# Building the key and query stacks of an attention kernel through DRAM: six stores and eight loads a unit in place of 24 pieces

## The chip, the cores and the metric

The kernel runs on one core of one Trainium2 chip. The metric is the device time of one execution in microseconds (us), the median of several runs. The profile is one execution taken by the hardware profiler; its span runs from the first instruction to the last. The engines are named as in the profile: PE (matrix multiplication; PEld its weight loads), DVE (vector), ACT (scalar functions), POOL (GpSimd) and SP, which here only issues DMA transfers. "SPq" is SP's queue of such issues.

## The reference, cut to what matters

One block of a transformer on x of 2048 tokens by 1024 columns. The part that matters is the first half, causal attention in four segments of 512 tokens, with a running memory from segment to segment, 32 heads of 32 columns:

```
q, k, v = LN(x) @ wq, LN(x) @ wk, LN(x) @ wv        # then cut into 32 heads, 4 segments of L = 512
for s in range(4):
    logits = einsum("bhqd,bhkd->bhqk", q[s], k[s]) * scale + causal mask
    a_dot  = softmax(logits) @ v[s]
    a_mem  = (phi(q[s]) @ M) / (phi(q[s]) @ z)
    o[s]   = g * a_mem + (1 - g) * a_dot
    M, z   = M + phi(k[s]).T @ v[s],  z + sum(phi(k[s]))
h  = x + concat(o) @ wo
h2 = h + gelu(LN(LN(h)) @ w1 + b1) @ w2 + b2
```

Everything is float32.

## The kernel before, in words

Matrix products are made with operands that are split into a high and a low part (names ending in h and l; the low part is the value less the high part), so that a product is three matmuls: high by high, low by high, high by low (`mm3`, lines 114 to 117).

The attention is done in two halves of two segments each. In a half the loop of lines 648 to 664 runs over 8 groups of 4 heads and, in each, over the two segments: 16 units a half, 32 in all. A unit is one call of `dense` (line 402): the projections of keys, queries and values for one group of heads and one segment, each 8 steps of three matmuls of 512 columns (lines 115 to 117). The tiles have the 128 columns of the group, 32 for each head, as partitions, and the 512 tokens as columns. While a unit's projections run, the four heads of the unit before are worked off: `interleave` (line 661) takes one step of `heads` after each step of `dense`. The steps of one head are written out in `PLAN` (line 31): `q` is the product of queries and keys (`qk`, line 533), `n` the normalisation of the softmax on POOL, `t` the transposes, `a` the product with the values, `s` and `o` subtractions and sums. The first step of a head's slot is a `q`, so the first `q` of a unit's heads follows the first step of the next unit's key projection.

The product of queries and keys is one matmul over 96 partitions: for head j a tile `ks` of 96 rows holds the head's 32 rows of kh, of kl and of kh again, and a tile `qs` holds qh, qh and ql, so that the sum over 96 rows is kh qh + kl qh + kh ql (line 541). These are the stacks. `stack` (line 372) makes the four tiles of a unit, called for the keys at the first step of the query projection (line 420) and for the queries at the first step of the value projection (line 435). kh and qh come from ACT (lines 413 and 427), kl and ql from DVE (lines 414 and 428). The tiles `ks` and `qs` have five buffers each: of the four tiles of a unit the first takes a free one, and each of the others waits until the product of queries and keys of one head of the unit before has read its buffer.

In the kernel before, each 32 rows of a stack tile are a DMA of its own from SBUF to SBUF (line 377): 4 tiles of 3 pieces for the keys, and the same for the queries, 24 pieces of 64 KB in a unit.

All DMAs around the change are issued on SP, whose queue runs in order: the pieces; the weights of the next groups (`load_block`, line 326, 512 KB each, two buffers; a buffer comes free when POOL or DVE has made the low part of the weights before it); the finished output rows of a group (line 609, `o_dram`, 256 KB each, from a tile of 128 by 512); at the end of a half those rows read back (line 683, `orr`), weights of the output projection (line 700) and rows of x (line 696). An instruction waits on SP for what it depends on, and all behind it waits too.

The program is written in a tile framework. It finds the dependences between instructions, tiles in DRAM included, and at build time a planner fixes the order of each engine's instructions and of each queue: it walks through the program with costs of its own and takes the earliest written instruction whose inputs it expects to be there. Around the attention only the opening (line 286) has its order written out by hand; elsewhere an instruction or a transfer may stand ahead of one that was written earlier but that the planner expects to be held up.

Of the kernel before, what the change touches and what calls it, by code (L numbers as in the profile page):

```python
# [10 lines left out]
F32 = mybir.dt.float32  # L11
# [6 lines left out]
P = 128  # L18
# [21 lines left out]
def raw(ap):  # L40
    return ap.bitcast(F32)


def build(tc, x, wq, wk, wv, wo, beta, w1, b1, w2, b2, out):
    nc = tc.nc
    top = ExitStack()
    const = top.enter_context(tc.tile_pool(name="const", bufs=1))
    dram = top.enter_context(tc.tile_pool(name="dram", bufs=1, space=DRAM))
# [33 lines left out]
    p1_dram = [dram.tile([P, 512], F32, name=f"p1_dram{j}") for j in range(FB // 2)]  # L82
    h_dram = [[dram.tile([S // P, P, FB // 4, P], F32, name=f"h_dram{i}{s}") for s in range(2)] for i in range(2)]

    acts = {}

    def split(pool, w, hi, lo, hi_eng="vector", lo_eng="gpsimd"):
# [99 lines left out]
    def hooked(gen, fn, every, count):  # L187
        for n, _ in enumerate(gen):
            if n % every == every - 1 and n // every < count:
                fn(n // every)  # L190
            yield
# [152 lines left out]
    def attention(half, first):  # L344
# [26 lines left out]

        def stack(a, b, name, order):
            out = []
            for j in range(4):
                st = ab.tile([96, 512], F32R, tag=name, name=name, bufs=5)
                for blk, src in enumerate(order):
                    nc.sync.dma_start(raw(st[32 * blk:32 * blk + 32, :]), raw((a, b)[src][32 * j:32 * j + 32, :]))
                out.append(st)
            return out

# [21 lines left out]
        def dense(g, sl, ws, u):  # L402
# [15 lines left out]
            for c in project(ws["q"], sl, "qps", qps):  # L418
                if c == 0:
                    u["ks"] = stack(kh, kl, "ks", (0, 1, 0))  # L420
                if c == 2 and s < 3:
                    zc = ab.tile([P, 64], F32, name="zc", bufs=2)[:, 0:1]
                    pk = phi_sum(kparts, "pk", zc)
                next(behind, None)
                yield
# [7 lines left out]
            for c in project(ws["v"], sl, "vps", vps):  # L433
                if c == 0:
                    u["qs"] = stack(qh, ql, "qs", (0, 0, 1))
                if s > 0:
                    if c == 2:
                        pq = phi_sum(qparts, "pq")
                    if c == 4:
                        while small:  # L440
                            one_small()
                        pqh, pql = tmpr("pqh"), tmpr("pql")
                        mzh = ab.tile([P, 256], F32R, name="mzh", bufs=1)[:, 0:132]
                        mzl = ab.tile([P, 256], F32R, name="mzl", bufs=1)[:, 0:132]
                        nc.scalar.copy(pqh, pq)
                        nc.gpsimd.tensor_copy(mzh, MZ[:, g, :])
                        nc.gpsimd.tensor_tensor(mzl, MZ[:, g, :], raw(mzh), op=ALU.subtract)
                    if c == 5:
                        nc.gpsimd.tensor_tensor(pql, pq, raw(pqh), op=ALU.subtract)
                if c == 1 and s < 3:  # L450
                    pkn = ps_dense("pkn")
                    for i in range(4):
                        nc.tensor.transpose(pkn[:, i * P:(i + 1) * P], pk[:, i * P:(i + 1) * P], ident)
                    pkh, pkl = tmpr("pkh"), tmpr("pkl")
                    nc.scalar.copy(pkh, pkn)
                if c == 2 and s < 3:
                    nc.vector.tensor_tensor(pkl, pkn, raw(pkh), op=ALU.subtract)
                next(behind, None)
                yield
# [188 lines left out]
        for g in range(NG):  # L648
            for sl in range(2):
                u = {"g": g, "s": 2 * half + sl}  # L650
                d = dense(g, sl, ws, u)
# [6 lines left out]
                else:  # L658
                    if g == NG - 1 and sl == 1:
                        d = hooked(d, lambda k: load_o(half, 0, k, ab), 3, NG - 1)  # L660
# [19 lines left out]
    def load_o(half, sl, g, tp):  # L680
        oh, ol = o_tiles(half, sl)
        orr = tp.tile([P, 512], F32, tag="tmp", name="orr", bufs=5)
        nc.sync.dma_start(orr, o_dram[2 * half + sl][g])
        hi, lo = oh[:, g, :], ol[:, g, :]
        if sl == 0 and g % 2 == 0:
            nc.vector.tensor_copy(hi, orr)
        else:
            op = nc.scalar.copy(hi, orr)
            if sl == 1:
                tc.add_manual_dep(op.ins, acts["mm"].ins.name, NOSYNC, reason="program order")  # L690
        (nc.vector if g % 2 else nc.gpsimd).tensor_tensor(lo, orr, raw(hi), op=ALU.subtract)
# [613 lines left out]
    for half in range(2):  # L1305
# [53 lines left out]
        order = ExitStack()  # L1359
# [84 lines left out]
```

## Time and profile before

| what | value |
|---|---|
| runs | 2302.54, 2304.96, 2303.82 us; median 2303.82 us |
| span of the profiled execution | 2296.2 us; the median of the runs is 7.6 us above it |
| PE busy | 2270.4 us, 99% of the span |
| DVE, ACT, POOL busy | 67%, 53%, 48% |
| granted clock of PE | 1.000 |
| attention, half 0 | about 30 to 500 us, then its output projection |
| attention, half 1 | about 900 to 1375 us, then its output projection |
| transfers on SP's queue | 316.40 MB, 45.4% of the 16 DMA engines' time over the span |
| pieces of the stacks | 768, 64.0 KB each, median 2.0 us from issue to landing |

The profile gives no time for its own execution other than the span; what lies around it is taken from the median of the runs. A share of busy time is a mean over stages. The rows that name a line group all instructions of that line: how often, how long, and how long the engine idled ahead of them. The ends of matmuls are modelled, since matmuls are pipelined: their starts follow each other faster than their durations say.

### The profile page before, as it was taken

What the parts mean: (1) busy time and instruction counts of PE and PEld (TensorE: products, weight loads), DVE (VectorE), ACT (ScalarE), POOL (GpSimd) and SP (SyncE); (2) the same over time, 40 slices, a digit from 0 to 9 for tenths busy, and PEclk for the clock granted to TensorE, in tenths of its full rate; (3) what the DMA queues carried; (4) which work ended last, traced back from release to release, by engine and by line L of the source; (5) the groups of instructions that cost most, each with busy time, mean ns of one, the idle gap of its engine ahead of it and who ended that gap; (6) DMA issues with size and microseconds to landing.
All of it is one profiled execution on the core that took longest, in us unless ns stands there. A gap on an engine that the chain in (4) does not pass through costs nothing.

```text
span 2296.2 us, 35279 instructions
## 1 busy us (share of the span) xinstructions
PE 2270.4 (99%) x11769; PEld 1890.8 (82%) x11769; DVE 1540.3 (67%) x3173; ACT 1225.0 (53%) x2549; POOL 1092.4 (48%) x1134
## 2 busy tenths in 40 slices
PE   8999999999999999999999999999999999999999
PEld 6888888878888888888888887888888888888887
DVE  6777777776655565777777777565566766577563
ACT  6777777775453445777777776363344223322221
POOL 5545555555244442555555556253445554155430
PEclk9999999999999999999999999999999999999999
DMA  6333333345465654433333344466667976476762
GB/s 190 92 85 91 93 89 85 87 120 182 139 204 172 188 165 142 113 91 86 85 87 88 87 111 140 156 211 175 176 188 263 345 243 216 159 253 221 249 234 90
DMA packets 322719, 355.36 MB, mean 155 GB/s; under 512 B 26190, under 2 KB 218730, under 8 KB 322538
## 3 DMA queue, kind: packets, MB, share of 16 engines
q1 hardware_dynamic: 259370, 316.40, 45.4%
q10 hardware_dynamic: 63168, 36.71, 5.3%
q8 instruction: 93, 1.52, 0.3%
q14 instruction: 88, 0.72, 0.1%
HBM read 226.59 MB, written 76.09 MB: 132 GB/s over the span
## 4 chain that ended last, share of the span: by engine, by line
PE 91%; ACT 3%; POOL 2%; DVE 2%; issue 1%; DMA 1%; ACTq 0%; SPq 0%; POOLq 0%; DVEq 0%
PE po L1278 22%; PE bps L882 9%; PE cps L882 7%; PE dps L882 6%; PE po L593 6%; PE ppt L573 6%; PE pqk L541 3%; PE vps L116 2%; PE vps L115 2%; PE kps L115 2%; PE kps L116 2%; PE vps L117 2%; PE kps L117 2%; PE pwo L117 2%; PE pwo L116 2%; PE pwo L115 2%
## 5 line engine op out<-in xcount | busy, mean ns | idle before, releaser
L557 POOL TENSOR_SCALAR pr<-pr,nm,gate 128x128 f32<-128x128 f32 (+3 forms) x512 | 322.6, 639 | 345.9 <-DVE nm L554 260.0
L550 ACT ACTIVATE pr<-pr,mx 128x256 f32<-128x256 f32 (+3 forms) x512 | 287.6, 562 | 161.9 <-DVE mx L542 158.2
L580 DVE TENSOR_TENSOR ptl<-ppt,pth 128x512 fp32r<-128x512 f32 (+1 forms) x384 | 227.2, 599 | 86.2 <-ACT pth L575 82.0
L542 DVE CUSTOM_DVE_ANT_0 pr<-pqk,mask 128x256 f32<-128x256 f32 (+3 forms) x512 | 243.3, 484 | 46.5 <-PE pqk L541 43.7
L573 PE MATMUL ppt<-ident,pr 128*128 128x128 f32 x1280 | 223.6, 277 | 2.1 <-POOL pr L557 1.4
L575 ACT CAST pth<-ppt 128x512 fp32r<-128x512 f32 (+1 forms) x384 | 194.2, 517 | 39.0 <-PE ppt L573 33.1
L1288 DVE TENSOR_TENSOR c<-c,po 128x512 f32<-128x512 f32 x160 | 105.4, 683 | 143.1 <-PE po L1278 135.5
L573 PEld LDWEIGHTS ppt<-ident,pr 128*128 128x128 f32 x1280 | 164.6, 140 | 32.5 <-POOL pr L557 2.6
L541 PE MATMUL pqk<-ks,qs 96*128 96x256 f32 (+3 forms) x512 | 161.3, 315 | 0.0
L92 POOL TENSOR_TENSOR wl<-wr,wh 128x1024 fp32r<-128x1024 f32 x52 | 124.5, 2393 | 70.8 <-PE pqk L541 27.6
L593 PE MATMUL po<-pth,vs 128*64 128x512 f32 (+3 forms) x512 | 155.4, 326 | 0.3 <-ACT pth L575 0.2
L593 PE MATMUL po<-ptl,vs 128*64 128x512 f32 (+3 forms) x512 | 153.9, 310 | 1.3 <-DVE ptl L580 1.2
L1278 PE MATMUL po<-w2h,zh 128*128 128x512 f32 x378 | 121.1, 390 | 0.8 <-DVE zh L1218 0.4
L1135 POOL TENSOR_TENSOR w2r<-w2r 128x512 f32<-128x512 f32 x54 | 85.4, 1593 | 72.0 <-DVE c L1288 36.9
L541 PEld LDWEIGHTS pqk<-ks,qs 96*128 96x128 f32 x512 | 96.2, 188 | 21.5
L994 POOL TENSOR_TENSOR s<-r 128x512 f32<-128x512 f32 x28 | 43.6, 1559 | 143.4 <-DVE sa L1010 87.1
L882 PE MATMUL bps<-zh,sb 128*128 128x512 f32 x336 | 111.0, 391 | 0.0
L882 PE MATMUL bps<-zh,sa 128*128 128x512 f32 x336 | 110.8, 390 | 0.0
L115 PE MATMUL vps<-yh,wh 128*128 128x512 f32 x256 | 109.4, 427 | 0.9 <-DVE MZ L497 0.9
L115 PE MATMUL kps<-yh,wh 128*128 128x512 f32 (+1 forms) x264 | 110.1, 417 | 0.0
L115 PE MATMUL qps<-yh,wh 128*128 128x512 f32 x256 | 106.8, 417 | 0.0
L1278 PE MATMUL po<-w2h,hl 128*128 128x512 f32 x322 | 103.2, 390 | 0.5 <-POOL hl L1218 0.3
(241 smaller groups left out, 6657.1 us busy)
## 6 DMA issues: line engine op xcount, KB each, us to landing
hr<-h_dram SPq DMA_DIRECT2D x112, 448.0 KB, 5.4
w2r<-in_B_w SPq DMA_DIRECT2D x122, 256.0 KB, 4.4
r<-in_B_w SPq DMA_DIRECT2D x56, 512.0 KB, 4.5
h_dram<-ht ACTq DMA_DIRECT2D x84, 256.0 KB, 3.7
ks<-kh SPq DMA_DIRECT2D x256, 64.0 KB, 2.0
qs<-qh SPq DMA_DIRECT2D x256, 64.0 KB, 2.0
wr<-in_A_wo SPq DMA_DIRECT2D x32, 512.0 KB, 4.0
wx<-in_B_w SPq DMA_DIRECT2D x56, 256.0 KB, 3.5
```

The lines of the kernel that those rows point to most:

```text
L115: nc.tensor.matmul(ps, ah, bh, start=first, stop=False)
L116: nc.tensor.matmul(ps, ah, bl, start=False, stop=False)
L541: nc.tensor.matmul(pqk[:, :n], u["qs"][j][:, i * P:(i + 1) * P], u["ks"][j][:, 0:n], start=True, stop=True)
L542: nc.vector.tensor_tensor_reduce(out=st["pr"][:, offs[i]:offs[i] + n], in0=pqk[:, :n], in1=mask[:, 512 - n:512], op0=ALU.add, op1=ALU.min, ...
L550: nc.scalar.activation(pi, pi, AF.Exp, bias=mx[:, i:i + 1], scale=-1.0, accum_out=mx[:, 4 + i:5 + i])
L557: nc.gpsimd.tensor_scalar(pi, pi, nm[:, 4 + k:5 + k], gate[:, 1, 4 * g + j:4 * g + j + 1], op0=ALU.mult, op1=ALU.mult)
L573: nc.tensor.transpose(ppt[:, o:o + P], pr[:, offs[i] + jk * P:offs[i] + (jk + 1) * P], ident)
L575: acts["pth"] = n, nc.scalar.copy(pth[:, base:base + w], ppt[:, :w])
L580: nc.vector.tensor_tensor(o, x0, x1, op=ALU.subtract)
L593: nc.tensor.matmul(po[:, P * jk:], v, st[part][:, koff[jk]:koff[jk] + w], start=(jk, part) == (0, "pth"), stop=(jk, part) == (2, "ptl"))
L882: nc.tensor.matmul(ps, x_[:, c, :], y_[:, c, :], start=first and c == 0 and n == 0, stop=last and c == 3 and n == 2, skip_group_check=True)
L1278: nc.tensor.matmul(ps, x_[:, k], y_[k], start=opens and k == 0 and i == 0, stop=closes and k == self.KP - 1 and i == 2, skip_group_check=True)
```

## The change

Four tiles in DRAM are added, two for the key stacks and two for the query stacks, used in turn. Each holds 128 rows of 3 parts of 512 columns, laid by row, then part, then column. `stack` first stores the three parts of all four heads, each with one DMA of 128 rows of 2 KB (256 KB, rows 6 KB apart in DRAM). Then each tile of 96 rows is loaded with one DMA: 32 rows of 3 parts lie together in DRAM, so that it is one stretch of 192 KB. In the tile, row 3r + p now holds part p of row r, where it was row 32p + r; keys and queries are permuted alike. Each load depends on all three stores. The calls of `stack` stay where they are, and all 14 transfers are issued on SP.

```diff
+    s_dram = {n: [dram.tile([P, 3, 512], F32, name=f"{n}_dram{k}") for k in range(2)] for n in ("ks", "qs")}
     acts = {}
...
         def stack(a, b, name, order):
             out = []
+            n = acts[name] = acts.get(name, 0) + 1
+            d = s_dram[name][n % 2]
+            for blk, src in enumerate(order):
+                nc.sync.dma_start(d[:, blk], raw((a, b)[src]))
             for j in range(4):
                 st = ab.tile([96, 512], F32R, tag=name, name=name, bufs=5)
-                for blk, src in enumerate(order):
-                    nc.sync.dma_start(raw(st[32 * blk:32 * blk + 32, :]), raw((a, b)[src][32 * j:32 * j + 32, :]))
+                nc.sync.dma_start(raw(st), d[32 * j:32 * j + 32].rearrange("r b n -> (r b) n"))
                 out.append(st)
             return out
```

## The prediction

> **What bounds the kernel now.** I read the page first: the span, the busy shares, the chain of work that ended last, and the group of the matmuls that read the stacks.
>
> ```profile
> span 2296.2 us, 35279 instructions
> ...
> PE 91%; ACT 3%; POOL 2%; DVE 2%; issue 1%; DMA 1%; ACTq 0%; SPq 0%; POOLq 0%; DVEq 0%
> ...
> L541 PE MATMUL pqk<-ks,qs 96*128 96x256 f32 (+3 forms) x512 | 161.3, 315 | 0.0
> ```
>
> PE carries 91% of the chain, DMA 1%. The last figure of the third row is what matters here: the 512 matmuls that read the stacks left PE idle before them for 0.0 us in all. A stack never comes late today. Then the windows, cut by stage: two rows of start, attention of half 0 and its end, and the start, attention and end of half 1. The columns are the window, its length, the busy time of PE, of its weight loads, of DVE, ACT and POOL (instructions in brackets), the granted clock, the DMA engines' share and GB/s.
>
> ```profile
> 0.00:30.00 30.00, 20.36 (x119) 17.74 (x119) 21.53 (x45) 17.34 (x24) 18.00 (x37) 1.00 0.73 223
> 30.00:60.00 30.00, 29.55 (x169) 24.47 (x168) 20.94 (x55) 20.38 (x50) 14.95 (x22) 1.00 0.57 159
> 60.00:480.00 420.00, 419.07 (x2554) 354.66 (x2554) 312.65 (x925) 305.09 (x774) 214.92 (x302) 1.00 0.34 87
> 480.00:560.00 80.00, 76.01 (x418) 61.21 (x417) 58.76 (x142) 53.71 (x119) 48.17 (x54) 1.00 0.46 143
> 920.00:960.00 40.00, 39.08 (x239) 32.86 (x240) 29.20 (x88) 26.65 (x69) 24.61 (x32) 1.00 0.46 126
> 960.00:1320.00 360.00, 360.00 (x2202) 305.35 (x2201) 273.04 (x813) 266.12 (x673) 203.44 (x267) 1.00 0.34 87
> 1320.00:1420.00 100.00, 96.32 (x561) 78.86 (x560) 75.97 (x205) 74.11 (x175) 54.19 (x67) 1.00 0.38 111
> ```
>
> PE is busy 419.07 of 420 us and 360.00 of 360 us in the two stretches where nearly all stacks are made, at full granted clock. In the stages that hold stacks (30 to 560 and 920 to 1420) PE idles 0.45 + 0.93 + 3.99 + 0.92 + 0.00 + 3.68 = 10.0 us. That is all that any change of these copies could win while PE's work stays as it is. The 9.6 us idle of the first 30 us lie ahead of the first query stack. So the question is not how much the copies get cheaper but whether they still arrive in time.
>
> **The deadline.** Each unit (one group of heads in one segment; 32 in all) makes a key stack and, one projection later, a query stack. The query stack is the one short of time: its first reader is the first matmul of the next unit's heads. One of the tight units, from the timeline of SP, ACT, DVE, POOL and PE:
>
> ```profile
> 1055.28 0.59 ACT L427 CAST qh<-qps 128x512 fp32r<-128x512 f32 x1
> 1056.50 0.67 DVE L428 TENSOR_TENSOR ql<-qps,qh 128x512 fp32r<-128x512 f32 x1
> 1055.51 2.40 POOL L92 TENSOR_TENSOR wl<-wr,wh 128x1024 fp32r<-128x1024 f32 x1 [1.47 <-PE pqk L541]
> 1054.68 0.51 SPq L377 DMA_DIRECT2D ks<-kh  x1
> ...
> 1064.15 0.53 SPq L326 DMA_DIRECT2D wr<-in_A_wk  x1
> 1064.28 0.28 PE L541 MATMUL pqk<-ks,qs 96*128 96x256 f32 x1
> ```
>
> ql is finished at 1056.50 + 0.67 = 1057.17 and PE reads the stack at 1064.28: **7.1 us**. Worked out in the same way for all 32 units, the time from ql to the first reader is 7.1 us in six units, 7.5 to 7.6 in seven, 8.0 to 8.1 in fourteen, 7.8 to 9.5 in three at the ends of the halves, and less in two, the first unit of each half (5.2 and 6.3). The last of the fourteen, and the first unit of all:
>
> ```profile
> 1332.56 0.69 DVE L428 TENSOR_TENSOR ql<-qps,qh 128x512 fp32r<-128x512 f32 x1
> 1341.30 0.28 PE L541 MATMUL pqk<-ks,qs 96*128 96x256 f32 x1
> ```
>
> ```profile
> 33.11 0.68 DVE L428 TENSOR_TENSOR ql<-qps,qh 128x512 fp32r<-128x512 f32 x1
> 38.97 0.28 PE L541 MATMUL pqk<-ks,qs 96*128 96x256 f32 x1
> ```
>
> **The change part by part.** Removed per unit: 24 pieces of 32 rows from SBUF to SBUF. Added: 6 stores of 128 rows, 8 loads of 96 rows, and a wait on SP between each three stores and their four loads. PE, ACT, DVE and POOL lose and gain no instruction; the rows of both stacks are permuted alike, so the products are the same sums. The prices, by line of issue: instructions of SP (min, median, max ns) and landing.
>
> ```profile
> L377 SPq DMA_DIRECT2D qs<-qh x256: 507/589/764, 33.4 to 1372.0; - x128
> DMA to landing us min/median/max: 1.9/2.0/4.9
> ...
> L609 SPq DMA_DIRECT2D o_dram<-ot x28: 332/463/527, 81.8 to 1359.5; - x28
> DMA to landing us min/median/max: 2.0/2.3/3.9
> ...
> L683 SPq DMA_DIRECT2D orr<-o_dram x28: 319/382/1153, 469.1 to 1414.1; - x28
> DMA to landing us min/median/max: 2.5/3.2/6.9
> ...
> DMA packets 128, 0.25 MB, mean 351 GB/s; under 512 B 8, under 2 KB 8, under 8 KB 128
> ```
>
> The nearest row for a store is o_dram<-ot (256 KB, 128 rows of 2 KB, SBUF to DRAM: the same shape), for a load orr<-o_dram (256 KB back; ours has 192 KB). The packet row is the DMA engines while one o_dram store moves its data: at 351 GB/s, 256 KB keep all 16 engines for 0.75 us. By the same rate a weight load of 512 KB keeps them for an estimated 1.5 us.
>
> SP's own time falls from 24 x 0.58 = 13.9 us a unit to 6 x 0.46 + 8 x 0.38 = 5.8 us. PE does not wait for SP, so this alone is worth 0.
>
> The chain of the query stack in the tight unit, after the change: the last key tile (which waits, as before, for a reader of the previous unit) costs SP one load instead of three pieces, so SP is free at 1055.1; the two qh stores go at 1055.9 and 1056.4, the ql store at about 1057.2. Three stores keep the engines for 3 x 0.75 = 2.25 us, begun at least 1.3 us before the third is issued, so the third is hardly held up; its median 2.3 us stands: 1059.5. Then the first load, 3.2 us: **1062.7**, 1.6 us ahead of PE's 1064.28. Bounds: with both minima (2.0 and 2.5) 1061.7, with both maxima (3.9 and 6.9) 1068.0, 3.7 us late. I take the medians, since the rows have 28 transfers each and the maxima belong to the crowded ends of the halves. In the 7.5 us and 8 us units the same chain of 5.5 us leaves 2.0 and 2.5 us. The other three loads follow 0.4 us apart and their heads come some 7 us later each.
>
> What gets between: SP's queue is in order, but the planner may place other transfers while the loads wait. The weight load of 1064.15 stood behind the pieces, though the POOL subtraction that frees a buffer ended at 1055.51 + 2.40 = 1057.91. If it goes between stores and loads it takes 1.5 us of engine time ahead of them and 0.5 us of SP: the six tight units, with 1.6 us in hand, would be between 0.1 us early and 0.4 us late. I book 0.1 us for each, 0.6 us (bounds 0 and 6 x 0.4). Behind SP's two waits stand otherwise only o_dram stores and loads of weights for a later group, which nobody needs within 2.3 us.
>
> Start: in the first unit 33.79 + 5.5 = 39.3 against 38.97: 0.3 us late, bounds -0.7 and +5.6. Half 1 starts with 6.3 us and fits. Bytes: the stack's 1.57 MB a unit now move twice, 6 x 0.75 = 4.5 us of all engines for the stores and at the same rate 4.5 us for the loads, 9 us of a unit of 30.8 us. Even on top of the share of 0.34, which holds the pieces that go, that makes 0.63.
>
> Sum: 0.6 + 0.3 = +0.9 us on the span of 2296.2 gives 2297.1. The runs shown have a median of 2303.82, 7.6 us above the span of the profiled execution; I keep these 7.6 us and round to **2305 us**.
>
> **The planner as cover.** The order of PE is made at build time by a planner that lets a matmul pass one whose data it expects late. The first unit of half 1 shows it: pieces for its head 0 are issued until 910.36 + 0.53.
>
> ```profile
> 910.36 0.53 SPq L377 DMA_DIRECT2D qs<-ql  x1
> ...
> 912.72 0.39 PE L116 MATMUL kps<-yl,wh 128*128 128x512 f32 x1
> 912.95 0.34 PE L541 MATMUL pqk<-ks,qs 96*128 96x256 f32 x2
> ```
>
> The stack matmul stands between the second and third matmul (lines 116 and 117) of a projection step, where the rows above have it behind a whole step: 912.95 is half a microsecond after 910.36 + 2.0, and 0.23 us after the matmul ahead of it, so PE did not idle for it. So lateness that the planner foresees costs next to nothing; only lateness that it does not foresee stalls PE, since PE's queue is in order. If this cover were gone, the price is the lateness itself, unit by unit.
>
> **Rivals.** (1) *The round trip through DRAM doesn't fit* (slower). Place: PE ahead of the first matmul of head 0. It decides from 7.1 us between ql and landing. At 8.0 us, which is the slowest store seen (3.9), a median load and 0.9 us of queue, six units lose 0.9 us and seven about 0.5, and the two starts 2.8 and 1.7: 13 us, about 2317. If the three stores were held one behind another, the chain is 1055.9 + 3 x 2.3 + 3.2 = 1066.0, 1.7 us late here and about 1.4 in the wide units: near 48 us, 2352, less what the planner reorders. For it: every unit has this chain and the margin is 1.6 us. Against: the medians fit, and the planner covers what it foresees. [...]
>
> (2) *SP's relief is worth something* (faster). Weight loads stop queuing behind pieces, the buffers of the halves come free once three stores have landed, and the 10.0 us idle shrink. Half of that is -5 us, 2299; all of it 2294. Against: not one idle time of PE in those stages is ended by a DMA by the page's groups, and the ends idle on the softmax chain.
>
> (3) *Only the order shifts.* A different plan moves units between two patterns that are both there:
>
> ```profile
> 66.29:128.21 61.92, 61.79 (x377) 52.27 (x376) 46.04 (x137) 44.91 (x115) 32.20 (x46) 1.00 0.37 95
> 971.77:1033.35 61.58, 61.58 (x378) 52.18 (x376) 46.59 (x140) 45.44 (x117) 34.72 (x47) 1.00 0.34 86
> ```
>
> Two units take 61.92 us in half 0 and 61.58 in half 1. Seven such pairs going the other way are 7 x 0.34 = 2.4 us: 2301.4 or 2306.2.
>
> **How the numbers follow.** Hidden, as forecast: 0.45, own range 2302 to 2308. Order shift (3): 0.15, of which 0.08 within 0.2%, 0.05 beyond it on the slow side, 0.02 on the fast. Rival (1): 0.29. Rival (2): 0.11. A measurement of this kernel can tell about 0.2%, 4.6 us, from no change. Faster 0.11 + 0.02 = 0.13; same 0.45 + 0.08 = 0.53; slower 0.29 + 0.05 = 0.34. The range reaches down to half of rival (2) and up to rival (1) at 8 us: 2299 to 2317; left out are the upper part of (1), with 0.13, and the lower of (2), with 0.05.
>
> **What would show it.** Right: PE busy stays above 419 of 420 and 359.5 of 360 in the two attention stretches; the stack matmuls' idle stays near 0; the ql store lands some 2.3 us, the first load 5.5 us after ql. Rival (1): idle of PE or its weight loads ahead of the stack matmuls, released by a DMA of ks or qs, once a unit, or SP rows with one store per 2.3 us. Rival (2): less idle at 480 to 560 and 1320 to 1420. Wrong altogether: PE itself slower with the heavier DMA traffic, which no row suggests (clock 1.00 at a DMA share of 0.73).

## The result and the profile after

The changed kernel takes 2323.28 us (median of 4 runs, 2320.90 to 2329.52) against 2304.39 us of the kernel before, 18.9 us more, where 2305 us were forecast and the range ended at 2317. The comparison of the runs gives a ratio of 1.0095, 95% interval 1.0076 to 1.0113 (the two medians by themselves 1.0082); the ratios below are made in the same way. The profiled execution took 2322.13 us, with a span of 2320.3 us, 24.1 us longer than the span before. An execution takes 1.7 to 1.9 us more than its span in all runs whose spans are on record, so the profiled execution before took an estimated 2298 us, some 6 us less than the median of its runs: the two spans overstate the loss by about 5 us.

From the page of the changed kernel, the same rows as in the prediction, and the queue that carries the copies (packets, MB, share of 16 engines; 316.40 MB and 45.4% before):

```profile
span 2320.3 us, 34605 instructions
...
PE 2277.5 (98%) x11769; PEld 1893.6 (82%) x11769; DVE 1539.1 (66%) x3173; ACT 1225.7 (53%) x2549; POOL 1093.2 (47%) x1134
...
q1 hardware_dynamic: 278826, 366.71, 49.4%
...
PE 88%; DMA 3%; ACT 3%; DVE 2%; POOL 2%; issue 1%; SPq 0%; ACTq 0%; POOLq 0%; DVEq 0%
...
L545 PE MATMUL pqk<-ks,qs 96*128 96x256 f32 (+3 forms) x512 | 162.2, 318 | 2.0 <-DMA qs<-qs_dram 1.8
```

Line numbers of the changed kernel are up to 4 higher than before, those of the experiments' kernels up to some 16. The last row is the surprise: in the whole kernel PE waited 1.8 us for a stack. Yet its idle time is 2320.3 - 2277.5 = 42.8 us instead of 25.8, and it is busy 7.1 us longer with the same 11769 matmuls. Where both lie, the windows of the changed kernel show (columns as in the prediction):

```profile
0.00:30.00 30.00, 20.13 (x118) 17.42 (x119) 21.43 (x45) 17.06 (x24) 17.50 (x36) 1.00 0.77 238
30.00:60.00 30.00, 25.46 (x133) 20.36 (x132) 16.33 (x44) 15.88 (x40) 9.51 (x15) 0.94 0.72 230
60.00:480.00 420.00, 418.81 (x2550) 353.94 (x2549) 311.13 (x920) 304.05 (x772) 217.94 (x306) 1.00 0.44 137
480.00:560.00 80.00, 73.14 (x406) 59.28 (x405) 57.78 (x147) 54.74 (x125) 41.19 (x50) 0.96 0.43 135
920.00:960.00 40.00, 35.96 (x197) 29.38 (x196) 23.21 (x69) 22.71 (x57) 18.48 (x23) 0.96 0.59 184
960.00:1320.00 360.00, 360.00 (x2204) 305.08 (x2203) 271.92 (x812) 264.12 (x669) 200.38 (x269) 1.00 0.43 135
1320.00:1420.00 100.00, 92.06 (x552) 75.60 (x551) 75.22 (x217) 73.69 (x181) 57.22 (x69) 1.00 0.48 152
```

The two long stretches, with 28 of the 32 units, are as they were: 418.81 of 420 and 360.00 of 360 us, while the DMA share rose from 0.34 to 0.44 and 0.43. Of the 17.0 us by which the idle time grew, 14.3 stand in the starts (30 to 60 and 920 to 960: idle 4.5 and 4.0 us, before 0.5 and 0.9) and in the ends (480 to 560 and 1320 to 1420: 6.9 and 7.9, before 4.0 and 3.7). In three of these four the granted clock is below 1.00, which it never was there before: there are four stretches of 3.41 us at half rate (granted clock 0.50), at 52.4, 506.4, 523.5 and 936.5 us. At half rate each costs an estimated 1.7 us, half of its length, 6.8 us in all; they make the 7 us of busy time.

What PE waited for, from its list of waits (us in total, times, longest), in the changed kernel:

```profile
PE ppt L577 <- POOL pr L561: 6.8, 6, 2.9
PE po L597 <- DVE ptl L584: 3.2, 3, 2.3
PE ppt L577 <- DVE ptl L584: 3.0, 3, 1.5
PE pom L520 <- DVE om L488: 2.2, 3, 1.5
```

and in the kernel before:

```profile
PE ppt L573 <- POOL pr L557: 1.4, 4, 0.5
PE po L593 <- DVE ptl L580: 1.2, 3, 0.5
...
PE pom L516 <- DVE om L484: 0.8, 1, 0.8
...
PE ppt L573 <- DVE ptl L580: 0.4, 1, 0.4
```

These four waits grew by 11.4 us. Three are steps of the softmax chain behind the stacks, on other engines (`pr` the normalised weights, `ptl` the low part of their transpose); `om` is the read of the running memory, which needs no stack. The transfers themselves, from the rows of the stores of both stacks (60 to 480 us), of the loads of the query stack (960 to 1320) and of the query stores of the first unit (30 to 36):

```profile
DMA to landing us min/median/max: 2.0/2.5/4.3
```

```profile
DMA to landing us min/median/max: 2.5/3.7/4.7
```

```profile
DMA to landing us min/median/max: 5.6/5.6/5.6
```

2.5 us for a store is near the 2.3 taken, 3.7 us for a load half a microsecond over the 3.2. Unit by unit, the first query tile lands 5.3 to 7.4 us after ql in the 28 inner units, whose readers come 7.0 to 9.3 us after it. In the first units of the halves it lands 9.2 and 8.7 us after ql, in the last ones 8.9 and 7.9.

### The profile page after: what moved, and what is told of

Its sections match the earlier page's. It is cut to its first block, busy times and chain, and to the rows that moved or that the text cites. A ratio compares the mean times of both kernels' runs of the same rounds, so it can differ in the third digit from the quotient of the medians.

```text
span 2320.3 us, 34605 instructions
## 1 busy us (share of the span) xinstructions
PE 2277.5 (98%) x11769; PEld 1893.6 (82%) x11769; DVE 1539.1 (66%) x3173; ACT 1225.7 (53%) x2549; POOL 1093.2 (47%) x1134
## 4 chain that ended last, share of the span: by engine, by line
PE 88%; DMA 3%; ACT 3%; DVE 2%; POOL 2%; issue 1%; SPq 0%; ACTq 0%; POOLq 0%; DVEq 0%
PE po L1282 20%; PE bps L886 10%; PE cps L886 7%; PE dps L886 6%; PE po L597 6%; PE ppt L577 6%; PE pqk L545 3%; PE pwo L118 2%; PE pwo L116 2%; PE pwo L117 2%; PE kps L117 2%; PE kps L116 2%; PE kps L118 2%; PE vps L116 2%; PE vps L117 2%; PE vps L118 2%
```

## The experiments

My theory at first was that of the windows: the loss lies in the four units at the ends of the halves, where 512 KB transfers stand around the trip through DRAM. The rivals: it is spread over all units; it comes from the order of other transfers and not from the trip. Every run has the kernel before beside it on its chip (medians 2301.3 to 2302.5 us); "above" means above that. The edits are shown shortened, against the changed kernel or the run named before them.

### Where: the inner units alone, the outer units alone

```diff
+            through = n - 1 not in (0, 15, 16, 31)      # the second run: "in"
             for blk, src in enumerate(order):
-                nc.sync.dma_start(d[:, blk], raw((a, b)[src]))
+                if through:
+                    nc.sync.dma_start(d[:, blk], raw((a, b)[src]))
```

The loads follow the same condition, and all other units keep the pieces.

> Stacks go through DRAM in 28 units; in the first and the last unit of each half (0, 15, 16, 31) the 24 pieces of the kernel before stay. Theory 'ends': in the inner units the round trip is over 5.3 to 7.4 us after ql, ahead of PE's first reader at 7.0 to 9.3 us, so nothing is lost there and the time goes back to that of the kernel before, within 3 us: 2302 to 2307. Rival 'everywhere' (the doubled bytes and SP's waits cost something in every unit): 28 of 32 shares of the 19 us remain, 2319 to 2322.

> Stacks go through DRAM in units 0, 15, 16 and 31 alone, all others in pieces. Theory 'ends': the whole loss, 2319 to 2326, with stretches of half granted clock near 52, 506, 523 and 936 us as in the changed kernel. Rival 'everywhere': 4 of 32 shares of 19 us, 2306 to 2308.

Measured: DRAM in the 28 inner units 2301.04 us, ratio 0.9997 (0.9988 to 1.0006); in the four outer units 2324.55 us, 1.0098 (1.0082 to 1.0113). The four units are the whole loss, and 28 trips cost nothing that can be measured. They also win nothing: in these units SP's relief is worth 0. That says little of the prediction's rival (2), which looked for its gain in the idle time of the ends, where this run keeps the pieces.

### What: keys alone, and no trip at all

For keys alone the condition is `name == "ks"`; the rows of the two stacks then lie in different orders, so the logits are other numbers. For "no trip" all 14 transfers stay, but a load reads the stack of the unit before.

> Key stacks go through DRAM in all units, query stacks stay in pieces. The key stack is stored a projection earlier than the query stack and has some 10 us more. Theory 'the query stack's lateness at the ends': nothing lost, 2302 to 2308. Rival 'the order of other transfers on SP' (SP's waits on landed stores let the planner move loads of weights, x and o_dram rows, and engines then wait for these): a part is lost here too, since half of SP's waits are here, 2308 to 2316.

> All stores and all loads stay, on SP in the same order, but the loads of a unit read the stack that the unit before stored (the first unit loads pieces), so that no load waits for a store to land: same bytes, no round trip. The kernel computes the heads with the wrong unit's stacks. Theory 'round trip': the loads land some 3 us after ql and the time is that of the kernel before within 4 us, 2301 to 2308. Rival 'bytes' (twice the bytes in the queues of the DMA engines make other transfers late): the loss stays, 2316 to 2324.

Measured: keys alone 2313.47 us, 1.0050 (1.0034 to 1.0065), and in its profiled execution, the fastest of the four, no half-rate stretch and a loss at the ends but hardly at the starts (PE idle 5.8 us in 480 to 570 against 4.0 before, 8.3 in 1320 to 1450 against 3.7). Without the trip 2308.40 us, 1.0035 (1.0024 to 1.0047). So about two thirds of the loss need the trip. What the rest is stays unclear: the first unit of the second run had pieces and stores one behind the other, and 30 to 60 us of its profile lost 3.9 us (idle time and half rate together) against the kernel before.

### Starts and ends apart, with what stands in the way held back

```diff
-            nc.sync.dma_start(hts[t], x[0, r0:r0 + P, :])
+            ld = nc.sync.dma_start(hts[t], x[0, r0:r0 + P, :])      # behind the unit's last query load on SP
+            if sl == 0:
+                tc.add_manual_dep(ld.ins, acts["got", "qs", 16 * half + 1].ins.name, NOSYNC, reason="program order")
```

For the ends the same hold goes to the read-backs of output rows (`load_o`), which are written down after the query stack.

> The stacks go through DRAM only in the first unit of each half (units 0 and 16); all other units keep the pieces. Theory (the loss lies in the four units where 512 KB transfers stand around a round trip): about half of the whole loss, since PE idle and half-rate stretches of the run with the four units alone split into 14.6 us at the two starts and 14.8 us at the two ends: 14 us above the kernel before, about 2315; half-rate stretches near 51 and 937 us, none near 510. Rival (the four places feed each other, for example one late start shifts all that follows): well under or over half, below 2308 or above 2321.

> The stacks go through DRAM only in the last unit of each half (units 15 and 31). Theory: the other half of the loss, about 15 us above the kernel before, 2316; half-rate stretches between 505 and 530 us, none near 51 or 937; PE waits for the last step of the transposed softmax weights behind the split of rows read back. Rival (the ends lose only because the half began late): under 4 us, within 2306.

> As the run with the two first units through DRAM, but the eight loads of rows of x (512 KB each, which nobody needs before the end of the half) are held behind the loads of that unit's query stack in SP's queue. Theory (the 512 KB transfers in the way make the round trip long): the ql store lands about 2.3 to 3 us after ql instead of 5, the first query tile 5.5 to 7 us after it instead of 8.7 to 9.2, and most of the loss of the starts goes: 2302 to 2308. Rival A (the bare round trip is too long for the starts, whose margin before was 5.2 and 6.3 us): the loss stays within 3 us of the run without the hold, 2311 to 2318. Rival B (the loss is what the planner makes of the unit, since it foresees the late stack and moves head 0): landing gets shorter, but head 0 stays where the planner put it, 9 us after ql, and so does the time.

> As the run with the two last units through DRAM, but the seven read-backs of finished rows of the first segment (256 KB each) are written down after the query stack of the last unit and held behind its loads in SP's queue. Theory: the ql store no longer has them behind and around it and DVE has no split of a row read back ahead of the softmax chain, so the query tile lands 5.5 to 7 us after ql instead of 8.9, PE's gap near 506 goes and most of the loss of the ends: 2303 to 2308. Rival (the rows are now read back too late for the output projection, or the key stack's own round trip holds the unit up): the loss stays, 2312 to 2320, with PE idle moved to 515 to 560 us.

Measured: starts 2318.20 us, 1.0067 (1.0054 to 1.0079); ends 2314.12, 1.0051 (1.0038 to 1.0063): 16.3 and 12.2 us above, together more than the whole change. Starts with x held 2311.67, 1.0036 (1.0023 to 1.0048); ends with the read-backs held 2315.52, 1.0056 (1.0043 to 1.0070). So the loads of x are worth 6.5 us, less than expected, and holding the read-backs nothing: the first query tile of the last units still landed 8.3 and 8.0 us after ql, and the rows became late for the output projection, where PE now waited 4.6 us. In the starts the ql store still landed 4.3 and 6.2 us after its issue.

### Two theories that fell

I thought next that the unit's own key loads (768 KB) hold the query stores up in the starts, and that at the ends DVE's split of a row read back blocks the chain. The chain of waits of the changed kernel had shown just that (start, us, what; pieces of up to 0.07 us left out):

```profile
496.76 4.74 DMA orr<-o_dram
...
501.52 1.79 DVE oh L690
...
503.38 1.66 POOL ol L695
...
505.06 0.69 DVE pq L370
505.75 0.61 DVE ptl L584
...
506.41 0.58 PE po L597
```

Two runs took each thing away, and a third is the yardstick with pieces for the second:

```diff
-            through = n - 1 in (0, 16)
+            through = name == "qs" and n - 1 in (0, 16)      # x and the next wq, wv held behind the query loads
...
-        orr = tp.tile([P, 512], F32, tag="tmp", name="orr", bufs=5)
-        nc.sync.dma_start(orr, o_dram[2 * half + sl][g])
+        orr = acts["mask"] if sl == 0 else tp.tile([P, 512], F32, tag="tmp", name="orr", bufs=5)
+        if sl:
+            nc.sync.dma_start(orr, o_dram[2 * half + sl][g])
```

> In the first unit of each half the query stack alone goes through DRAM, keys by pieces, and nothing else is issued between its stores and loads: rows of x and the next weights of queries and values are held behind the loads. (The rows of its two stacks are then permuted differently, so the logits of these two units are other numbers.) Theory, after the hold alone left 10 of 16 us: the unit's own key loads (768 KB, issued 2 to 3 us ahead of the query stores because no heads lie between the projections in a first unit) hold the query stores up. Without them the ql store lands 2.3 to 3 us after ql, the first tile at 5.5 to 6, and PE loses no more than the excess over the 5.2 and 6.3 us that it had: 0 to 3 us, 2302 to 2306. Rival (it is the trip itself, or the planner's placing): the store still lands 4 us or more after ql, or PE still stands 1.8 and 3.7 us ahead of head 0, and the time stays near 2309 to 2312.

> As the run with the two last units through DRAM, but the seven read-backs of finished rows of the first segment are left out: the split takes a tile that lies in SBUF (so half of the output projection multiplies other numbers). To be compared with the next run, which leaves them out of the kernel with pieces. Theory (the rows read back land late behind the stacks' transfers, and DVE's split of them stands ahead of the softmax chain): the gap of 2.3 us ahead of a matmul of ptl and the half-rate stretch behind it go, and the difference between the two falls from 12 us to under 4. Rival (the unit's own two trips, and what the planner makes of them, hold the heads up): the difference stays at 8 to 13 us, with PE waiting for pr, om, pth or the stacks.

> The kernel before, with pieces everywhere, with the same seven read-backs left out (same other numbers in the output projection): the yardstick of the run ahead of it. Both theories: at or a little below the kernel before, 2297 to 2303, since its read-backs left PE idle for little.

Measured: starts 2311.74 us, 1.0046 (1.0031 to 1.0061); ends without read-backs 2314.81, 1.0055 (1.0043 to 1.0068); its yardstick 2301.66, 1.0001 (0.9993 to 1.0010). Both theories fell. At the starts the trip was now as short as forecast (2.5 us from issue to landing of the store, the first tile 5.9 us after ql in unit 0; in the first unit of half 1 the store was issued 3.8 us late, behind the key pieces, and the tile landed at 9.2), and 10.5 us were still lost. At the ends the row that ended last in the chain could go and 13.2 us stayed. The chain names one path; another of nearly the same length must have stood beside it.

### What it was at the starts: a subtraction on POOL

The timeline of POOL in the kernel before, first unit (pr is the normalisation of the softmax, wl the low part of the next group's weights):

```profile
41.17 0.98 POOL L557 TENSOR_SCALAR pr<-pr,nm,gate 128x128 f32<-128x128 f32 x2 [9.75 <-DVE nm L554]
44.35 1.94 POOL L557 TENSOR_SCALAR pr<-pr,nm,gate 128x384 f32<-128x384 f32 x2 [2.20 <-DVE nm L554]
46.26 2.39 POOL L92 TENSOR_TENSOR wl<-wr,wh 128x1024 fp32r<-128x1024 f32 x1
```

and in the changed kernel, with SP and PE:

```profile
33.21 0.82 SPq L378 DMA_DIRECT2D qs_dram<-qh  x2
34.12 0.43 SPq L378 DMA_DIRECT2D qs_dram<-ql  x1
35.42 0.98 SPq L700 DMA_DIRECT2D ht<-in_A_x  x2
39.91 1.73 SPq L381 DMA_DIRECT2D qs<-qs_dram  x4
...
43.35 0.42 PE L545 MATMUL pqk<-ks,qs 96*128 96x256 f32 x2 [1.24 <-DMA qs<-qs_dram]
...
46.10 0.98 POOL L561 TENSOR_SCALAR pr<-pr,nm,gate 128x128 f32<-128x128 f32 x2 [14.46 <-DVE nm L558]
47.77 2.35 POOL L93 TENSOR_TENSOR wl<-wr,wh 128x1024 fp32r<-128x1024 f32 x1 [0.69 <-PE qps L118]
50.11 2.81 POOL L561 TENSOR_SCALAR pr<-pr,nm,gate 128x384 f32<-128x384 f32 x4
...
51.26 0.33 PE L577 MATMUL ppt<-ident,pr 128*128 128x128 f32 x1 [2.94 <-POOL pr L561]
```

Head 0 is late, and now wl stands between its two pairs of normalisations instead of behind them. The second pair comes 2.35 us later, and PE, in order, stands 2.94 us ahead of the transpose that needs it. Then follows the half-rate stretch. In the first unit of half 1 wl stands between the pairs in the same way, and in the run with the query stack alone the same order of POOL was there, with 2.7 us on PE. So: put wl back behind the normalisations and touch nothing else.

```diff
+        low = split(pool, wr, wh, wl, hi_eng, lo_eng)
+        if c0 == P:                                     # acts["scaled"]: head 0's last normalisation
+            tc.add_manual_dep(low.ins, acts["scaled"].ins.name, NOSYNC, reason="program order")
```

> As the run with the two first units through DRAM and nothing else changed in their transfers, but on POOL the low parts of the next group's weights (2.4 us each) are held behind the four normalisations of head 0. Theory (a late head 0 lets the planner put a 2.4 us subtraction of weights between head 0's two pairs of normalisations on POOL's in-order queue; PE's order does not foresee it, so PE stands 2.9 and 2.3 us ahead of a transpose and its clock halves for 3.4 us): these two gaps go and the half-rate stretch after the first of them; what is left are the 1.4 and 2.8 us ahead of head 0 itself: 2305 to 2310 instead of 2318. Rival (the late stack costs its lateness however POOL is ordered): 2314 to 2320, PE waits as long, for another engine.

> As the run whose first units send only the query stack through DRAM with nothing in the way, with the same hold on POOL. (Logits of the first units permuted as there.) Theory: the two causes together are the whole loss of the starts, so 2301 to 2306, no gap of PE above 1.5 us in 30 to 60 and 905 to 960 us and no half-rate stretch there. Rival (something else in the unit is late as well): 2308 to 2313 as without the hold.

Measured: the starts with this hold alone 2307.49 us, 1.0023 (1.0012 to 1.0034); with the query stack alone and nothing in the way 2301.94, 1.0003 (0.9995 to 1.0012). What the starts lose falls from 16.3 us to 5.9, and from 10.5 to 0.4: one subtraction moved in each of the two first units is worth 10 us together. POOL and PE in the first of the two runs, first unit:

```profile
46.70 0.98 POOL L569 TENSOR_SCALAR pr<-pr,nm,gate 128x128 f32<-128x128 f32 x2 [14.00 <-DVE nm L566]
48.40 1.42 POOL L569 TENSOR_SCALAR pr<-pr,nm,gate 128x384 f32<-128x384 f32 x2 [0.71 <-DVE nm L566]
49.79 2.39 POOL L93 TENSOR_TENSOR wl<-wr,wh 128x1024 fp32r<-128x1024 f32 x1
```

```profile
43.95 0.42 PE L553 MATMUL pqk<-ks,qs 96*128 96x256 f32 x2 [0.77 <-DMA qs<-qs_dram]
...
49.12 0.33 PE L587 MATMUL ppt<-ident,pr 128*128 128x128 f32 x1 [0.20 <-POOL pr L569]
...
49.88 0.33 PE L587 MATMUL ppt<-ident,pr 128*128 128x128 f32 x1 [0.36 <-POOL pr L569]
```

The stack is nearly as late as without the hold; the 2.94 us have become 0.2. In the first unit of half 1 the same execution shows less:

```profile
922.85 0.66 PE L553 MATMUL pqk<-ks,qs 96*128 96x256 f32 x2 [3.64 <-DMA qs<-qs_dram]
```

There PE no longer stands ahead of the transposes (2.6 us without the hold), but 3.6 us ahead of head 0 instead of 2.8, since the first tile landed 11.8 us after ql instead of 10.9, and it ran at half rate for 6.8 us instead of 3.4. By idle time and time lost at half rate, the two starts (30 to 60 and 905 to 960 us) lose 4.5 us less in this pair of executions (10.8 instead of 15.2) and 9.9 less in the pair with the query stack alone (3.9 instead of 13.8). The medians agree in both pairs, but the place of the gain is seen in full in the second alone.

### What it was at the ends: loads of the output weights

At the ends ACT, with POOL or DVE for the low part, splits the weights of the output projection (wo), and their loads stand on SP between and behind the trips. ACT in the run without read-backs (stacks of the last units through DRAM):

```profile
509.10 1.05 ACT L92 CAST zh<-wr 128x1024 fp32r<-128x1024 f32 x1 [2.26 <-DMA wr<-in_A_wo]
510.06 0.40 ACT L560 ACTIVATE pr<-pr,mx 128x128 f32<-128x128 f32 x1
```

ACT stood 2.26 us for a load, with an exponential behind it; in its yardstick with pieces ACT has no such wait in this stretch, the first comes at 545 us. POOL in the same run, and then in the yardstick (zl is the low part of such weights):

```profile
502.91 2.39 POOL L93 TENSOR_TENSOR zl<-wr,zh 128x1024 fp32r<-128x1024 f32 x1 [1.83 <-ACT zh L92]
505.28 2.49 POOL L567 TENSOR_SCALAR pr<-pr,nm,gate 128x384 f32<-128x384 f32 x2
```

```profile
502.15 1.41 POOL L557 TENSOR_SCALAR pr<-pr,nm,gate 128x384 f32<-128x384 f32 x2 [1.57 <-DVE nm L554]
507.16 0.98 POOL L557 TENSOR_SCALAR pr<-pr,nm,gate 128x128 f32<-128x128 f32 x2 [3.60 <-DVE nm L554]
508.48 2.40 POOL L92 TENSOR_TENSOR zl<-wr,zh 128x1024 fp32r<-128x1024 f32 x1 [0.34 <-ACT zh L91]
```

As at the starts, a low part of 2.4 us went ahead of a pair of normalisations, here in the last units of both halves. (In the changed kernel itself, with the read-backs, zl stands behind these pairs as it did before; but there, too, ACT stands 2.1 and 1.7 us for a load of wo ahead of an exponential, near 517 and 1401 us, which it never does before the change.) The next two runs leave out, besides the read-backs, the loads of wo at the end of each half (the splits take a tile in SBUF), with the stacks of the last units through DRAM and with pieces.

```diff
+        if acts.get("ends"):
+            return acts["mask"][:, 0:1].unsqueeze(2).to_broadcast([P, 2, 512])
         wr = wp.tile([P, DC, P], F32, tag="wr", name="wr", bufs=2)
```

> As the run with the two last units through DRAM without the seven read-backs, and also without the loads of the output projection's weights in the end of each half: their splits take a tile in SBUF (so half of the output projection multiplies other numbers). To be compared with the next run. Theory, formed after the read-backs were shown innocent (ACT stood 2.3 us for a weight load of wo ahead of two exponentials, POOL made a low part of 2.4 us ahead of a normalisation): splits of weights, whose loads land late behind the trips, stand ahead of the softmax chain in in-order queues; without the loads the difference between the two runs falls from 13 us to under 4. Rival (head 0 to head 3 of the last unit start later by the trip and there is no dense work to hide it): 8 to 13 us remain.

> Pieces everywhere, with the same read-backs and the same loads of output weights left out: the yardstick of the run ahead of it. Both theories: 2295 to 2302; the splits are as many as before, only never late.

Measured: 2303.35 us, 1.0006 (0.9997 to 1.0015) and 2303.05, 1.0007 (0.9998 to 1.0016). Of 13.2 us remain 0.3. So without the read-backs the cause at the ends are those loads beside the trips. With the read-backs, as in the changed kernel, both stand in the way of the chain, and no run takes the loads alone away. Whether the loads act by making the trip long or by their late splits, one more run was to tell; it moves only the load that stood between the query stores and loads:

```diff
-        nc.sync.dma_start(wr, wo[k * 256:(k + 1) * 256, n * 512:(n + 1) * 512].rearrange("(c p) n -> p c n", p=P))
+        ld = nc.sync.dma_start(wr, wo[k * 256:(k + 1) * 256, n * 512:(n + 1) * 512].rearrange("(c p) n -> p c n", p=P))
+        if acts["first"] == 3:                  # the fourth load of wo in a half: behind the last query load on SP
+            last = acts["got", "qs", max(x_[2] for x_ in acts if x_[0] == "got")]
+            tc.add_manual_dep(ld.ins, last.ins.name, NOSYNC, reason="program order")
```

> As the run with the two last units through DRAM without the seven read-backs (2314.8 us; its yardstick with pieces 2301.7), but one transfer is moved: the 512 KB load of output weights that stood between the stores and loads of the query stack is held behind those four loads. Leaving all those loads out closed the gap between the two, which does not say why. Explanation A (it lengthens the trip: query tiles landed 8.6 us after ql with it and 5.2 without any): the tiles land at 5.3 to 6.5 and the time falls to 2302 to 2306. Explanation B (the splits of the weights stand on ACT and POOL ahead of the softmax chain and wait for loads that land late): the loads land later still, so 2310 to 2318, with ACT waiting for a load of wo ahead of an exponential.

Measured: 2308.00 us, 1.0029 (1.0018 to 1.0040), between the two. Loads of the last query stack (490 to 502 us), before and after the move:

```profile
DMA to landing us min/median/max: 5.3/5.6/5.6
```

```profile
DMA to landing us min/median/max: 2.6/3.3/4.1
```

The trip is short again and more than half of the loss is gone. But the split of that load moved too: ACT now waits 0.8 us for loads of wo in this stretch instead of 2.6, and POOL's low part falls behind a pair of normalisations that it had stood ahead of. The run moved both suspects, so their shares stay open.

### The whole change with the holds

> The whole change as it was made, with one thing added: POOL's low parts of the second group's weights are held behind the four normalisations of head 0 of each half. Theory: what the hold was worth with the two first units alone (2318.2 to 2307.5) it is worth here: 10 us less than the change, 2311 to 2315, no half-rate stretch near 52 us. Rival (in the whole change other things take its place): 2319 or more.

> The whole change with all the holds: POOL's low parts behind head 0's normalisations; rows of x and the next weights of queries and values behind the first unit's query loads; the fourth load of output weights behind the last unit's query loads. The read-backs and the key stacks' own trips stay as in the change. Theory: the starts lose 2 to 4 us (the key loads still delay the query stores), the ends 4 to 8: 2307 to 2313, not below the kernel before. Rival (the holds delay things that the halves' ends need): no better than with the POOL hold alone.

Measured: with the POOL hold 2316.33 us, 1.0064 (1.0051 to 1.0077): 13.8 us above where the change is 18.9 above, 5 us better by the medians and 7 by the ratios, of 10 expected, and without a half-rate stretch at either start; PE stands 1.7 us ahead of head 0 in the first unit of half 1. With all the holds 2310.18, 1.0040 (1.0026 to 1.0054), as expected; by idle time and half rate its profiled execution lost 3.9 us more than the kernel before at the starts and 9.1 at the ends (480 to 570 and 1320 to 1450 us), where the changed kernel lost 10.5, so the holds hardly reach the ends while the read-backs are there. No version was faster than the kernel before; the one with DRAM in the inner units equals it.

## Why the prediction was wrong, point by point

**Right.** The inner units. "ql store lands some 2.3 us, the first load 5.5 us after ql" came out as 2.2 to 4.0 and 5.3 to 7.4. The tight units, for which 0.6 us were booked because a weight load might get between, lost nothing measurable: a weight load did get between, and their tiles land 6.1 to 7.0 us after ql, with the reader at 7.1. Of the margin of 1.6 us between 0.1 and 1.0 was left; that it sufficed in all six is in part luck. The two conditions for "right" on the long stretches held but for 0.2 us in the first (418.81 for 419).

**Wrong: "Start: in the first unit 33.79 + 5.5 = 39.3 against 38.97: 0.3 us late".** The store took 5.6 us and the chain 9.2; half 1, which "starts with 6.3 us and fits", had its tile at 8.7. The bound of 5.6 us late was there, on the ground of the maxima, and I put the medians, since "the maxima belong to the crowded ends of the halves". But these units are the crowded ends: with the unit's own key loads, the rows of x and the next weights out of the way the store took 2.5 us. The price by runs: 16.3 us for the two starts, where 0.3 were booked.

**Wrong: "lateness that the planner foresees costs next to nothing".** It holds for PE's order: head 0 was moved from 5.2 to 9.3 us after ql and PE stood only 1.2 us for it. But a late head 0 also changes the order on POOL, where the planner used the hole for a subtraction of 2.4 us, and this cost more than the lateness: 10.4 of 16.3 us by the medians.

**Wrong: "loads of weights for a later group, which nobody needs within 2.3 us".** In the last unit the loads behind the trips are those of the output projection, and their splits are in the queues of ACT and POOL ahead of the softmax chain. The ends were not priced at all: 12.2 us by the run with them alone, and where the read-backs are out of the way, too, leaving these loads out takes 13.2 us down to 0.3.

**Missing: the clock.** 7 of the 24 us of span are matmuls at half rate behind the new gaps; the sum has no term for it.

**Readings.** The 7.6 us between span and median, which carry the sum from 2297.1 to 2305, are no constant: the executions on record lie 1.7 to 1.9 us above their spans, and the rest is that the profiled execution was a fast one. Adding them only gives the measured median back, so the sum takes no harm. Of the three units "at the ends of the halves" with 7.8 to 9.5 us, one is the second unit of half 1; nothing hangs on it.

**The rivals.** (1) named the right direction but not the place: of its mechanism, PE ahead of head 0, only 1.8 us are found in the changed kernel, and the widest part of its sum, 28 units late, did not happen. In the first unit the trip was 9.2 - 5.5 = 3.7 us longer than forecast, in the 28 inner ones, where it took 5.3 to 7.4 us, at most 1.9 us longer; with the transfers around it out of the way the first unit, too, came to 5.9 us. (2) won nothing in the inner units, and at the ends, where it looked for less idle time, that time grew from 7.7 to 14.8 us. (3) did not happen as priced: from head 0 to head 0 two units take 61.9 us in half 0 and 61.6 in half 1 in both kernels, with one stretch of 62.4 in half 0 of the changed one. An order that did shift, and cost, is that of POOL at the starts.

## What to carry to other kernels

A trip that fits in the steady state is to be priced again in the first and last unit of each loop with that stage's own landing times, since there the queue holds other large transfers (here a store took 5.6 us in the first unit, against a median of 2.5 in the inner ones of half 0) and the deadline is another (here 5.2 us against 7.1 to 8.1). Where the order of each engine's instructions is planned at build time, a late input is not paid once at its reader (here the order on POOL made 10.4 of the 16.3 us of the starts): look at what the planner puts into the hole on the other engines, and at which splits wait there for a load. And before a cause that the chain of waits names is believed, take it away: here the rows read back stood on the chain and were worth nothing (12.2 us lost at the ends with them, 13.2 without).

## What the runs showed of the hardware that was not expected

The four half-rate stretches of the changed kernel last 3.41 us each. They begin at 52.42, 506.39, 523.46 and 936.47 us; the last three starts lie 133, 138 and 259 times 3.413 us behind the first. In the 3.41 us just ahead of each PE idled for 2.61, 2.55, 2.15 and 2.35 us; after 1.47 us idle in as long a time, 1383.62 to 1387.03 us, full rate followed. The length of a single gap did not tell which would follow: in the starts with x held, one of 1.76 us that ended at 41.55 us was followed by a half-rate stretch (granted clock 0.94 in 30 to 60 us), and one of 3.68 us that ended at 921.85 us was not (1.00 in 900 to 960). How much idle time it takes was not shown. The windows just at and after such a stretch in the changed kernel (PE clock third from the right):

```profile
52.42:55.82 3.40, 3.40 (x14) 2.81 (x12) 1.47 (x4) 1.36 (x3) 0.85 (x3) 0.50 0.93 261
56.00:59.40 3.40, 3.40 (x23) 2.86 (x22) 1.90 (x7) 1.60 (x5) 1.17 (x2) 1.00 0.02 5
```

14 matmuls instead of 23 in 3.4 us.
